# Where the transposed keys of one batch are copied, and in which order the first half of the work is issued

## The chip, the cores and the metric

The kernel runs on one core of a Trainium2 chip. The metric is the device time of one execution in microseconds. Before the change four runs gave a median of 235.56 us (234.56 to 236.28).

## The reference

Two stages are joined. The first is attention with 4 batches, 8 heads, 768 tokens and 64 numbers per head. Three heads ("retrieval") see all earlier tokens; the other five ("streaming") see the first 4 tokens and a window of 64. The second is a dense layer pair with a learned slope for negative values.

```python
stream_keep = causal & (is_sink | in_win)
mask = np.where(retr[0, :, 0, 0, None, None], full_mask, stream_mask)
scores = np.where(mask[None, :, :, :], scores, -1000000000.0)
a = np.exp(scores)
a = a / (np.sum(a, axis=-1, keepdims=True) + 1e-09)
...
x = np.ascontiguousarray(attn_out.transpose(0, 2, 1, 3)).reshape(B * S, H * D)
h = x @ w_in
g = np.maximum(h, 0.0) + alpha * np.minimum(h, 0.0)
return (g @ w_out).astype(np.float32)
```

`w_in` is 512 x 2048, `w_out` 2048 x 512, and `x` has 3072 rows.

## The kernel before

The attention is cut into 16 **segments** of two heads each: segment n belongs to batch n // 4 and holds the pair PAIRS[n % 4] (line 99). The four batches follow each other, and the dense layers of a batch run beside the attention of the next. The work is written as named items, and one long list, ORDER (lines 14 to 71), says in which order they are issued. Each engine runs its own instructions in the order of this list and waits at each for what it needs; so an item that is late holds up all that is behind it on its engine. The names are:

- `Lq5`, `Lk5`, `Lv5`: loads of a segment's queries, keys and values, from SyncE's (SP's) DMA queue. `Cq`, `Ck`, `Cv`: their casts to bf16. Lines 300 to 302 give the engine of each by a letter: P is GpSimd (POOL), A ScalarE (ACT), V VectorE (DVE). For segments 0 to 5 most are on GpSimd.
- `Tq5`, `Tk5`: transposes on TensorE (PE) into a PSUM bank, for segments 0 to 7 (`to_array`, line 354). `tq5`, `tk5.0`, `tk5.1`: copies of these to SBUF, for each head of the keys (`put_q`, line 364, `put_k`, line 372). Segments 8 to 15 are transposed by DMA.
- `S5.0.1`: a part of the scores on PE (lines 410 to 427 and 498), `s5.0.1` its exp on ScalarE (lines 466, 514, 520), `m5.0.1` the mask after it on VectorE. `A5.0`: the product with the values on PE (line 553), `a5.0` its division (lines 563 and 564). `X5`, `x5`: transpose of the result and copy to xT.
- `P0.4`: columns of the first dense layer, x @ w_in (`P1`, line 589). t = 0, 2, ... are the 512 tokens at the head of a batch, t = 1, 3, ... the other 256. P0.0 to P0.5 are cut in three, so that they can start before all heads are ready. `p0.4` is the negative part (relu with a factor of -1 on ScalarE, line 603, written to neg), `g0.4` the rest on VectorE (line 610), which gives the bank back to PE.
- `O0.1.2`: a quarter of the second layer for 128 tokens (`P2`, line 614), `o0.1` its copy and store. `L` and `l` are the last ones.
- `wi0` to `wi7`: loads of w_in, `wo0` to `wo3`: loads of w_out, all issued by GpSimd (lines 704 to 711). wi0 and wi1 hold the first 512 columns (f = 0 to 3), wi2 and wi3 the next (f = 4 to 7), and so on, half of the rows in each.

PSUM has eight banks. An item that needs one takes the bank that has been free longest, by the order of the list (`take`, line 145), and waits for whoever read it last.

In `put_k` a retrieval head's keys are one copy of 64 x 768 (line 385). A streaming head's are three: a large one of 64 x 744 (line 389) and two small ones (64 x 20, line 390, and 64 x 28, line 391). For segments 1 to 3 all are on VectorE. For segments 4 to 7, batch 1, the large copy of head 0 is on ScalarE, all others are on VectorE.

Scores of segments 4 and later are collected and issued in a burst (`emit_burst`, line 414): the two heads of a pair lie in different halves of the array's rows, and when each half has 576 columns or more, their matmuls are mixed (line 427), so that they run at once; else each runs alone (line 420). What stands between two score items in the list decides which scores come into one burst (`beside_burst`, line 431).

Of the kernel before, what the change touches and what calls it, by code (L numbers as in the profile page):

```python
# [25 lines left out]
p0.10 s5.0.1 s4.0.0 S4.1.5 S4.0.5 g0.8 Lq6 g0.10 S4.1.0 S4.0.3 nz1 p1.12 g1.12 p0.13 s4.1.0 s4.0.3 P0.15 Ck6.0 Lv5
S4.0.4 kfz0 P1.6 g0.13 p0.7 g0.7 Ck7.0 S5.1.0 ms s4.0.4 O0.1.0 Ck6.1 mr Cv5 S5.1.1 s4.1.5 s5.1.0 S4.0.1 S5.0.2 s4.0.5
S4.1.1 m4.1.5 p0.15 s5.1.1 P0.14 P0.12 s5.0.2 s4.1.1 O0.1.1 p1.6 p0.14 g0.15 s4.0.1 kfz3 P1.14 S4.1.4 S4.1.2 g1.6
S4.0.2 g0.14 Lk8 S5.0.0 S4.1.3 p0.12 s4.0.2 m5.0.2 g0.12 s4.1.3 m4.1.0 m5.1.1 O0.1.2 s4.1.2 Lq8 Tk7 m4.0.0 P1.10 Tk6
s4.1.4 O0.0.0 Lv7 O0.1.3 Cq6 Tq6 m5.0.1 tk7.0 tk7.1 p1.14 m4.0.1 O0.3.0 p1.10 O0.0.1 tk6.1 g1.14 Lv4 g1.10 Cv4 Ck8  # L30
s5.0.0 Lv6 m5.1.0 Lk9 O0.3.1 m4.1.3 tq6 m4.0.4 tk6.0 S6.1.2 S6.0.5 o0.1 m5.0.0 S7.0.1 m4.1.4 S6.1.0 S5.1.2 S7.0.2
O0.0.2 m6.0.2 Cq8 s6.1.0 O0.3.2 A5.0 s6.1.2 m4.0.3 Dk8.0 s5.1.2 Cv7 O0.3.3 m14.0.2 ns O0.0.3 m5.1.2 A5.1 s7.0.1 a5.0
m4.0.5 a5.1 o0.3 s7.0.2 A4.0 O0.2.0 s6.0.5 o0.0 X5 S6.0.0 S7.1.2 S6.0.3 a4.0 S7.1.0 S6.0.4 S6.1.1 O0.2.1 x5 s6.1.1 Ck9
S6.0.1 S6.0.2 O0.2.2 s6.0.4 m6.1.0 m4.1.1 s6.0.3 S7.1.1 Lq9 S7.0.0 s6.0.1 s7.1.0 m4.0.2 Dq8 A4.1 O0.2.3 O1.1.0 Cv6
s7.1.1 Dk8.1 m7.0.2 s6.0.0 nr o0.2 Cq9 S8.0.2 S8.0.0 O1.1.1 m6.1.1 s7.1.2 m7.1.0 s6.0.2 m6.0.1 s8.0.2 s8.0.0 a4.1
s7.0.0 S8.1.5 m7.0.1 S8.0.4 S8.0.3 m6.0.5 S8.1.3 m6.0.4 m6.0.0 m7.1.2 m6.1.2 S8.1.4 S8.0.1 s8.0.3 O1.1.2 m6.0.3 s8.0.4
m8.0.0 S8.1.0 m7.0.0 A6.1 A6.0 O1.1.3 a6.1 s8.0.1 m7.1.1 s8.1.3 Dk9.0 a6.0 Dk9.1 A7.1 a7.1 s8.1.4 A7.0 a7.0 Dq9 O1.0.0
Lq11 s8.1.5 X6 X4 Lq10 x4 x6 m8.1.3 S9.1.0 S9.0.0 kfz2 X7 s8.1.0 O1.0.1 x7 near0 m8.0.1 s9.0.0 Cq10 o1.1 s9.1.0 S8.0.5
S8.1.1 S9.0.1 m9.0.0 S9.0.2 S8.1.2 S9.1.2 s9.0.2 P2.13 s9.0.1 Lk10 P3.4 s8.1.2 s8.0.5 Cq11 m8.0.5 m9.0.1 Lv8 p2.13
P2.7 near2 p2.7 P2.3 P2.1 g2.13 p2.3 m8.0.3 s9.1.2 Ck10 O1.0.2 s8.1.1 Lv9 Lk12 m8.1.4 g2.3 g2.7 p3.4 Dq10 Cv8 Dk10.1  # L40
P2.4 P2.0 g3.4 p2.4 m8.1.5 m8.0.4 p2.1 P2.5 p2.0 m8.1.0 g2.4 S9.1.1 P2.8 P2.9 p2.5 P2.2 Dk10.0 Lk11 g2.1 p2.9 g2.5
g2.0 Dq11 A8.0 g2.9 P2.6 Lv11 O1.0.3 near1 m8.1.1 p2.2 p2.8 a8.0 g2.8 P2.14 Lv10 P2.11 s9.1.1 p2.6 g2.2 p2.14 m9.1.1
o1.0 S10.1.2 S10.1.0 S10.0.1 g2.6 S10.0.5 S10.1.1 g2.14 S10.0.2 s10.0.5 m9.1.2 s10.1.1 p2.11 P2.15 Cv9 m9.0.2 s10.1.2
P3.14 s10.0.2 s10.1.0 P3.2 Lq12 Lk13 O2.2.0 A8.1 Ck12 Ck11 m9.1.0 Dk11.1 g2.11 S10.0.3 S10.0.4 p2.15 s10.0.1 p3.2
s10.0.4 g3.2 P2.10 A9.1 s10.0.3 g2.15 p2.10 P3.8 A9.0 m10.1.2 a8.1 g2.10 m10.1.1 m10.0.5 m10.0.3 p3.8 P2.12 Lq14
Dk11.0 P3.6 m10.0.1 P3.10 Dk12.1 a9.1 Cq12 p3.6 p3.10 m10.1.0 O2.2.1 P3.12 O2.2.2 g3.8 p3.14 a9.0 O2.1.0 O2.1.1 g3.6
g3.10 p2.12 p3.12 S10.0.0 O2.1.2 S11.1.1 S11.1.0 g3.14 S11.0.1 g2.12 S11.0.0 m10.0.4 s10.0.0 P3.0 Cv10 X8 Lq13 s11.0.0
m10.0.0 s11.1.0 m11.1.0 p3.0 s11.0.1 s11.1.1 O2.1.3 A10.0 Ck13 Dq12 S11.0.2 O2.3.0 s11.0.2 S11.1.2 o2.1 O2.0.0 Cv11
g3.0 s11.1.2 m11.0.1 Dk12.0 Cq13 Dk13.0 m11.1.1 g3.12 O2.2.3 O2.0.1 a10.0 m11.1.2 A10.1 A11.1 a10.1 m11.0.0 O2.0.2
O2.0.3 Dk13.1 a11.1 m11.0.2 S12.0.1 S12.1.4 o2.2 S12.1.0 S12.0.0 o2.0 A11.0 O2.3.1 s12.0.1 Dq13 S13.1.1 S13.1.0 a11.0  # L50
S12.0.4 s12.1.0 S12.1.2 S13.0.1 s12.1.4 m12.1.4 s12.0.0 S13.0.2 X9 X10 s13.1.1 X11 s12.0.4 s12.1.2 s13.1.0 x11 O3.1.0
Lk15 O2.3.2 m13.1.1 S12.0.3 S12.0.5 S12.0.2 s13.0.2 S12.1.1 m13.1.0 m12.0.4 s13.0.1 S12.1.5 S13.1.2 O3.1.1 s13.1.2
P4.0 s12.1.5 s12.0.2 Cq14 P4.11 P4.1 Lq15 m12.1.5 p4.11 Lk14 O2.3.3 p4.0 s12.0.5 m12.0.1 p4.1 s12.1.1 O3.1.2 s12.0.3
Ck15 m12.0.2 g4.11 P4.13 O3.0.0 g4.0 P4.12 P5.6 m13.1.2 p4.13 Ck14 Lv13 Lv15 g4.1 g4.13 p4.12 m12.0.3 P4.4 P5.2 g4.12
# [20 lines left out]
def kernel(  # L75
# [296 lines left out]
    def put_k(key, n, hh, both=False):  # L372
        h = heads(n)[hh]
        T = row_tokens(n, h)
        rows = slice(64 * hh, 64 * hh + 64)
# [4 lines left out]
        if put[key] == 1 + both:  # L380
            give(held.pop(key))
        if RETR[h]:
            cuts = [0, -(-256 // T), S // T] if n == 0 else [0, S // T]
            for lo, hi in zip(cuts, cuts[1:]):
                copy(kt[:, 0:S].rearrange("d (p t) -> d p t", t=T)[:, lo:hi, :], src[:, lo:hi, :])
# [3 lines left out]
        copy(slots[:, 0:6, a:last, :], src[:, first:z, :].rearrange("d (j m) t -> d j m t", j=6))  # L389
        nc.vector.tensor_copy(slots[:, 6, a:a + S // T - z, :], src[:, z:S // T, :])  # L390
# [466 lines left out]
```

## Time and profile before

| what | value |
|---|---|
| median of four runs | 235.56 us |
| the profiled execution | 235.06 us |
| its span, first to last instruction | 233.3 us |
| TensorE clock granted | 1.00 |
| ScalarE neg, 128x512 (line 603) | 96 times, 611 ns |
| VectorE g, 128x512 and 128x256 (line 610) | 742 and 474 ns, 64 each |
| VectorE kT, 64x768, 64x744, 64x20, 64x28 | 956, 924, 170, 179 ns |
| ScalarE kT, 64x768, 64x744 | 804, 778 ns |
| ScalarE, smallest activation (128x96, line 516) | 269 ns |

The profile is of one execution. Busy time is a share of an engine's span; an instruction's duration overlaps a little with the next one's, so the step from one start to the next is shorter where an engine has work waiting. "A <- B" in a list of waits means that A's engine stood idle until B had ended. The chain of waits goes back from the last instruction: at each step to what released it. A line of it has the start, the length and what it was.

### The profile page before, as it was taken

To read this page: it belongs to the slowest core of one execution; us is meant where nothing else is said; L and a number is where in the kernel's file an instruction comes from. 1 tells how busy PE (TensorE), PEld (TensorE's weight loads), DVE (VectorE), ACT (ScalarE), POOL (GpSimd) and SP (SyncE) were. 2 spreads that over 40 slices of the span, in tenths; PEclk is the share of its full clock that TensorE was granted. 3 is DMA by queue.
4 is the path that set the end of the run, shared out by engine and by line. 5 is a ranking of instruction groups with operands and counts; after the bars stand their busy time and mean duration, and the time that the engine had idled before them with its cause. 6 is when DMAs were issued, how large, how long until landed. Compare 5 with 4: busy or idle time off the path is not lost.

```text
span 233.3 us, 5251 instructions
## 1 busy us (share of the span) xinstructions
PE 223.8 (96%) x2011; PEld 137.1 (59%) x2011; DVE 158.4 (68%) x409; ACT 136.0 (58%) x266; POOL 46.8 (20%) x95
## 2 busy tenths in 40 slices
PE   7798999989999999999999999999999999999994
PEld 6587757545656575556665546556764555554553
DVE  5776749698788797998977476978880245545110
ACT  6598419798856758677563864589422333623231
POOL 3679469002058110000001000010000020000000
PEclk9999999999999999999999999999999999999999
DMA  6999999999999999999959999680310130110033
GB/s 197 322 217 172 239 280 236 215 198 200 206 225 194 208 211 219 162 203 217 191 108 139 251 205 207 116 212 3 71 35 0 49 135 1 45 48 0 0 135 136
DMA packets 90833, 36.23 MB, mean 155 GB/s; under 512 B 77864, under 2 KB 89016, under 8 KB 90808
## 3 DMA queue, kind: packets, MB, share of 16 engines
q1 hardware_dynamic: 84616, 26.59, 58.9%
q0 software_dynamic: 5728, 8.91, 17.1%
q10 hardware_dynamic: 464, 0.40, 0.5%
q8 instruction: 15, 0.25, 0.5%
q14 instruction: 10, 0.08, 0.1%
HBM read 27.55 MB, written 6.29 MB: 145 GB/s over the span
## 4 chain that ended last, share of the span: by engine, by line
PE 77%; DMA 9%; DVE 6%; issue 2%; ACT 2%; POOL 1%; SPq 1%; DVEq 0%; POOLq 0%
PE P L618 33%; PE P L598 30%; PE P L553 5%; DMA w_in_b<-in_moe_w_in_dram 5%; DVE g L610 4%; PE P L427 3%; DMA qf<-in_q_dram 2%; DMA vf<-in_v_dram 2%; PE P L420 2%; PE P L637 2%; PE P L578 1%; DVE kT L389 1%; ACT neg L603 1%; PE P L362 1%; ACT qT L367 1%
## 5 line engine op out<-in xcount | busy, mean ns | idle before, releaser
L610 DVE SCALAR_TENSOR_TENSOR g<-neg,oma,P 128x512 bf16<-128x512 f32 (+1 forms) x128 | 72.1, 608 | 36.3 <-ACT neg L603 35.6
L598 PE MATMUL P<-xT,w_in_b 128*128 128x256 bf16 (+1 forms) x512 | 92.1, 326 | 1.0 <-DVE g L610 0.8
L603 ACT ACTIVATE neg<-P 128x512 f32<-128x512 f32 x96 | 55.8, 611 | 59.2 <-PE P L598 51.3
L618 PE MATMUL P<-w_out_b,g 128*128 128x512 bf16 x368 | 88.5, 379 | 0.0
L598 PEld LDWEIGHTS <-w_in_b 128*128 128x128 bf16 x512 | 48.5, 98 | 34.5 <-issue 2.2
L618 PEld LDWEIGHTS <-g 128*128 128x128 bf16 x368 | 34.5, 98 | 35.9 <-issue 0.8
L466 ACT ACTIVATE eR<-P 128x448 bf16<-128x448 f32 (+6 forms) x63 | 36.4, 630 | 7.7 <-PE P L459 3.1
L628 POOL DMA_DIRECT2D out_dram<-ot x18 | 10.4, 578 | 124.1 <-ACT ot L624 124.1
L624 ACT COPY ot<-P 128x512 f32<-128x512 f32 x23 | 13.2, 589 | 13.3 <-PE P L618 10.1
L564 DVE TENSOR_TENSOR xn<-P,rcp 128x448 bf16<-128x448 f32 (+1 forms) x32 | 19.4, 608 | 1.1
L520 ACT ACTIVATE eS<-P 128x384 bf16<-128x384 f32 (+1 forms) x25 | 13.6, 567 | 6.0 <-PE P L498 2.4
L514 ACT ACTIVATE eS<-P 128x352 bf16<-128x352 f32 x30 | 13.9, 488 | 4.2 <-PE P L420 2.3
L410 PE MATMUL P<-qT,kT 128*128 128x192 bf16 (+12 forms) x68 | 11.2, 251 | 1.3 <-ACT eR L466 0.8
L553 PEld LDWEIGHTS <-eS 128*128 128x128 bf16 x260 | 10.2, 97 | 3.4 <-issue 1.1
L553 PE MATMUL P<-vb,eS 128*128 128x65 bf16 x260 | 11.1, 193 | 0.9 <-POOL vb L310 0.9
L563 DVE RECIPROCAL rcp<-P 128x7 f32<-128x7 f32 (+1 forms) x32 | 6.3, 198 | 7.4 <-PE P L553 7.3
L529 DVE TENSOR_TENSOR eS<-eS,ms_near 128x352 bf16<-128x352 bf16 x30 | 9.8, 334 | 1.6 <-ACT eS L514 1.3
L347 POOL CAST vb<-vf 128x896 bf16<-128x896 f32 x6 | 5.6, 933 | 25.4 <-DMA vf<-in_v_dram 25.4
L553 PEld LDWEIGHTS <-eR 128*128 128x128 bf16 x276 | 9.7, 97 | 1.5 <-DVE xn L564 0.3
L553 PE MATMUL P<-vb,eR 128*128 128x65 bf16 x276 | 10.3, 193 | 0.1
L427 PE MATMUL P<-qT,kT 64*128 64x176 bf16 (+17 forms) x159 | 9.7, 247 | 0.4 <-DVE g L610 0.3
L427 PEld LDWEIGHTS <-kT 64*128 64x128 bf16 x159 | 6.3, 94 | 6.2 <-issue 5.4
(97 smaller groups left out, 189.4 us busy)
## 6 DMA issues: line engine op xcount, KB each, us to landing
out_dram<-ot POOLq DMA_DIRECT2D x18, 256.0 KB, 3.2
vf<-in_v_dram SPq DMA_DIRECT2D x22, 192.0 KB
kf<-in_k_dram SPq DMA_DIRECT2D x21, 192.0 KB
qf<-in_q_dram SPq DMA_DIRECT2D x18, 192.0 KB
qf<-in_q_dram SPq DMA_DIRECT2D x7, 384.0 KB
w_in_b<-in_moe_w_in_dram POOLq DMA_DIRECT2D x8, 256.0 KB, 9.5
w_out_b<-in_moe_w_out_dram POOLq DMA_DIRECT2D x4, 512.0 KB, 15.4
kf<-in_k_dram SPq DMA_DIRECT2D x9, 196.0 KB
```

The source lines that it names most:

```text
L410: nc.tensor.matmul(to, keys, queries, start=True, stop=stop)
L427: nc.tensor.matmul(to, keys[own], queries[own], start=True, stop=True)
L466: nc.scalar.activation(ebuf[n, hh][:, lo:hi].rearrange("p (x c) -> p x c", x=len(parts)), P[:, got[0]:got[0] + len(parts), 0:(hi - lo) // ...
L514: nc.scalar.activation(slots, sc[:, 0:352].rearrange("p (s c) -> p s c", c=176), AF.Exp, scale=scale)
L520: nc.scalar.activation(slots, sc.rearrange("p x (s c) -> p x s c", c=192), AF.Exp, scale=scale)
L553: nc.tensor.matmul(pav[:, i, :], e[:, o:o + 128], vv[:, j, hh, 0:D + 1], start=(m == 0), stop=(m == len(terms) - 1))
L564: nc.vector.tensor_tensor(xn[n][:, 0:nt, D * hh:D * hh + D], pav[:, :, 0:D], rcp.to_broadcast([128, nt, D]), op=ALU.mult)
L598: nc.tensor.matmul(psg[:, w * i:w * (i + 1)], w_in_b[:, c, 128 * fb:128 * (fb + 1)], xT[:, c, o:o + w], start=(x == 0), stop=(x == 3))
L603: nc.scalar.activation(neg[t, f], bank(held["P", t, f][0]), AF.Relu, scale=-1.0)
L610: nc.vector.scalar_tensor_tensor(g_buf[t % 2][:, fb, 0:w], neg[t, f][:, c], oma[:, fb:fb + 1], bank(got[0])[:, c], op0=ALU.mult, op1=ALU.add)
L618: nc.tensor.matmul(bank(held["O", t, s][0]), g_buf[t % 2][:, f, 128 * s:128 * (s + 1)], w_out_b[:, f, :], start=(f == 0), stop=(f == 15))
L624: nc.scalar.copy(ot, bank(got[0]))
```

## The change

In `put_k` all three copies of a key now use the engine of the segment: ScalarE for segments 4 to 7, both heads and small copies too, and VectorE for segments 0 to 3.

ORDER is another list up to the middle of batch 2 (lines 15 to 53); from the item P4.0 on it is as before. The same items are in it. The first lines of both, up to the first items of the second layer, and the code:

```diff
-kz0 id La zero Lq0.0 Lk1 kz1 vz0 Lk0 Lq1 Lq0.1 Lq3 vz1 sz0 Cq0.0 ro nmr qz0 kz2 kfz1 warm0 Ck1.0 Tq0.0 warm1 Ck1.1
-Ck0.0 Lq2 Tk0.0 warm2 tk0.0 tq0.0 Ck0.1 Tk0.1 S0.0.1 vz2 s0.0.1 idf Lk2 sz1 one Cq1 Cq0.1 Lv0 Tk1 S0.0.2 Lk3 Tq0.1
-s0.0.2 nms tk0.1 tk1.0 Lv1 Cq2 S0.0.0 s0.0.0 Tq1 tq0.1 tq1 S0.1.2 tk1.1 qz sz2 Ck2.0 S0.1.0 Ck2.1 Lv2 s0.1.2 wi0
-m10.0.2 Tq2 s0.1.0 Cv0 S1.0.1 s1.0.1 Tk2 S0.1.1 S1.1.0 vz3 vo Lv3 A0.0 s0.1.1 s1.1.0 S1.0.0 tk2.1 A0.1 tq2 Ck3.1 kz3
-tk2.0 Ck3.0 S2.0.0 a0.0 Tk3 a0.1 Cq3 s1.0.0 S2.1.0 wi1 s2.0.0 Cv1 s2.1.0 so X0 Lq4 wi3 wi2 S1.1.1 tk3.0 Tq3 x0 s1.1.1
-S2.0.1 tq3 A1.1 S2.0.2 tk3.1 s2.0.1 A1.0 a1.1 s2.0.2 Cv2 S3.1.0 s3.1.0 A2.0 S2.1.1 Cv3 a1.0 a2.0 Lk5 S3.1.1 X1 s2.1.1
-S3.0.0 Cq4 x1 A2.1 s3.1.1 S3.0.1 A3.1 a2.1 P0.1.0 wi5 s3.0.1 P0.0.0 a3.1 X2 s3.0.0 wi4 x2 P0.3.0 wi6 A3.0 a3.0 P0.0.1
-P0.3.1 wi7 P0.2.0 P0.1.1 Al Lk4 Ck5.1 P0.2.1 al X3 x3 Ck5.0 P0.4.0 P0.4.1 P0.5.0 P0.3.2 P0.2.2 p0.3 P0.5.1 P0.0.2
-P0.4.2 p0.2 Ck4.1 Lq5 Tk5 P0.5.2 Cq5 Lq7 g0.3 p0.4 g0.2 P1.0 P0.1.2 g0.4 tk5.0 tk5.1 Tq4 p0.1 g0.1 p0.5 wo0 wo1 P0.6
-tq4 Lk7 P1.4 P1.2 p0.6 g0.5 Tq5 p1.4 g0.6 p1.0 Ck4.0 g1.4 p0.0 Tk4 g1.0 Cq7 P0.9 p0.9 P1.8 g0.0 p1.2 Tq7 tq7 P0.11
-p1.8 tq5 P0.8 tk4.0 g0.9 p0.11 tk4.1 wo2 g1.2 p0.8 wo3 P0.10 g1.8 P1.12 nz0 S5.0.1 S4.0.0 P0.13 Ck7.1 g0.11 P0.7 Lk6
...
+Lq0.0 zero La id qz nmr Lk0 kz1 sz2 kz2 Ck0.1 vo Lk1 nms Ck0.0 qz0 Lq0.1 Lq1 kz0 Cq0.0 warm0 Tq0.0 warm1 sz1 tq0.0 Lq2
+vz0 Cq0.1 Tk0.0 warm2 tk0.0 Lk2 S0.0.0 sz0 s0.0.0 Tk0.1 S0.0.2 Lv0 vz1 Cq1 s0.0.2 Lk3 tk0.1 Tq0.1 S0.0.1 Ck1.0 s0.0.1
+Tq1 Ck1.1 vz2 Ck2.0 Tk1 ro Cq2 tq1 tq0.1 vz3 S0.1.1 S0.1.2 Ck2.1 s0.1.1 S0.1.0 Tk2 tk1.0 Cv0 tk1.1 s0.1.2 S1.1.1 Tq2
+s1.1.1 so Ck3.1 A0.0 Lv1 s0.1.0 S1.0.1 tk2.1 S1.1.0 tq2 idf tk2.0 kz3 Lv2 Ck3.0 Lq3 A0.1 Cv1 s1.0.1 wi0 m6.0.2 s1.1.0
+a0.0 S1.0.0 Tk3 S2.0.2 wi1 s1.0.0 Lv3 Cq3 a0.1 Lk4 X0 tk3.0 s2.0.2 wi2 Cv2 A1.0 S2.1.0 s2.1.0 x0 A1.1 a1.0 Cv3 S2.1.1
+a1.1 Tq3 s2.1.1 S2.0.1 Ck4.0 X1 tk3.1 Lq5 tq3 S2.0.0 Ck4.1 A2.1 Lk5 mr m4.0.2 s2.0.1 s2.0.0 S3.1.0 x1 A2.0 S3.1.1
+s3.1.0 a2.1 s3.1.1 S3.0.0 wi3 A3.1 wi4 s3.0.0 S3.0.1 s3.0.1 a2.0 Lk6 Tk4 Lq6 X2 a3.1 x2 A3.0 P0.3.0 tk4.0 P0.2.0 Al
+a3.0 X3 Ck5.0 Cq5 x3 P0.0.0 tk4.1 wi5 wi7 P0.0.1 P0.2.1 P0.3.1 P0.1.0 Tq5 al Lq4 wi6 P0.2.2 P0.1.1 Lq7 P0.3.2 P0.1.2
+P1.0 ms P0.0.2 p0.3 P0.5.0 P1.6 g0.3 tq5 Ck6.1 p0.1 P1.4 P0.5.1 Ck5.1 P0.5.2 p0.0 g0.0 Lk7 g0.1 p1.6 g1.6 p0.2 P0.6
+P0.4.0 Tk5 Lv5 p0.5 wo0 g0.2 one P0.4.1 g0.5 p1.0 p1.4 Cq4 g1.0 p0.6 P0.11 Ck6.0 Lq8 P0.4.2 P1.2 g0.6 wo2 tk5.0 nr
+tk5.1 nz0 g1.4 p1.2 Tq4 P1.8 m10.0.2 P0.10 S5.1.2 g1.2 wo1 p1.8 kfz0 p0.4 g1.8 Lk8 kfz1 wo3 p0.11 P0.14 g0.4 Cq6 P0.13
...
@@ put_k @@
-        copy = cast_of("A" if n >= 4 and hh == 0 else "V")
+        copy, small = (cast_of(x) for x in ("AA" if n >= 4 else "VV"))
...
         copy(slots[:, 0:6, a:last, :], src[:, first:z, :].rearrange("d (j m) t -> d j m t", j=6))
-        nc.vector.tensor_copy(slots[:, 6, a:a + S // T - z, :], src[:, z:S // T, :])
-        nc.vector.tensor_copy(slots[:, :, 0:a, :], src[:, 0:a, :].unsqueeze(1).to_broadcast([64, 7, a, T]))
+        small(slots[:, 6, a:a + S // T - z, :], src[:, z:S // T, :])
+        small(slots[:, :, 0:a, :], src[:, 0:a, :].unsqueeze(1).to_broadcast([64, 7, a, T]))
```

More of the change, by code (lines that the diff above doesn't have):

```diff
@@ L25 @@
-p1.8 tq5 P0.8 tk4.0 g0.9 p0.11 tk4.1 wo2 g1.2 p0.8 wo3 P0.10 g1.8 P1.12 nz0 S5.0.1 S4.0.0 P0.13 Ck7.1 g0.11 P0.7 Lk6
[L26 to L54, printed above, removed]
+Lq0.0 zero La id qz nmr Lk0 kz1 sz2 kz2 Ck0.1 vo Lk1 nms Ck0.0 qz0 Lq0.1 Lq1 kz0 Cq0.0 warm0 Tq0.0 warm1 sz1 tq0.0 Lq2
@@ new lines @@
+tq4 p0.14 kfz3 p0.10 P0.9 P0.8 g0.11 p0.13 g0.14 Tq6 p0.9 g0.10 g0.13 P1.10 g0.9 P0.12 tq6 p0.8 g0.8 Cq7 p0.12 P0.7
+p1.10 P1.14 S5.1.1 p0.7 s5.1.2 g0.12 O0.0.0 S4.1.1 S4.1.4 Lv4 p1.14 Lq9 S4.0.0 g1.10 s5.1.1 S5.0.0 g0.7 g1.14 S4.0.1
+kfz2 s4.0.0 s4.1.1 P0.15 s4.0.1 m4.0.0 Ck7.1 m5.1.1 P1.12 m4.1.1 s4.1.4 S4.0.4 S5.1.0 p0.15 g0.15 s5.0.0 S4.1.3 S4.0.2
+O0.0.1 s4.1.3 s4.0.2 S5.0.2 S4.1.2 Tk6 Cv5 m5.1.2 p1.12 O0.1.0 Cv4 s5.0.2 m4.1.3 Lk9 m5.0.0 Cq8 Ck7.0 O0.1.1 O0.1.2
+s4.0.4 s4.1.2 tk6.1 tk6.0 s5.1.0 Ck8 m4.0.4 O0.0.2 S4.1.5 S4.0.5 S4.0.3 S4.1.0 S6.1.2 m5.0.2 m4.1.4 s4.0.3 s4.1.0
@@ new lines @@
+s4.1.5 m5.1.0 O0.1.3 s6.1.2 g1.12 m4.0.1 Tq7 S5.0.1 O0.0.3 A5.1 s4.0.5 O0.3.0 O0.3.1 o0.0 Tk7 m4.0.3 m4.1.5 a5.1
+s5.0.1 m4.0.5 m4.1.0 tk7.0 O0.3.2 A4.0 m5.0.1 o0.1 A4.1 tk7.1 Lv6 a4.0 Dk8.1 Dq8 tq7 a4.1 O0.3.3 o0.3 A5.0 a5.0 Lv7
+S6.0.5 S6.1.1 S7.1.1 S6.0.4 S6.1.0 S7.0.0 s7.0.0 Cq9 Cv6 s6.1.0 O1.1.0 s6.0.4 s6.1.1 S7.0.1 S6.0.3 X5 nz1 O0.2.0
+m6.0.4 s6.0.5 s7.0.1 S7.1.2 S6.0.1 x5 O1.1.1 s6.0.1 Ck9 s7.1.1 O1.1.2 S6.0.2 S8.1.0 m6.0.1 s7.1.2 S7.1.0 m7.0.0 s6.0.3
+S7.0.2 S6.0.0 m6.1.2 S8.1.5 O0.2.1 O0.2.2 Dq9 m6.1.1 m6.0.3 Dk9.0 s6.0.2 m7.0.1 m7.1.1 s6.0.0 s7.1.0 Dk8.0 m6.1.0
@@ new lines @@
+m6.0.5 s7.0.2 m7.0.2 Cv7 m6.0.0 A6.1 O0.2.3 A6.0 O1.1.3 m7.1.2 Dk9.1 ns s8.1.0 m7.1.0 Lk10 o0.2 Lq13 o1.1 a6.0 A7.1
+A7.0 O1.0.0 Lv8 a6.1 S8.1.4 s8.1.4 O1.0.1 s8.1.5 S8.0.0 S8.0.3 S9.1.0 S8.1.1 a7.0 S8.1.3 a7.1 S9.0.1 Lk11 Lk12 S9.0.0
+O1.0.2 s8.0.0 Ck10 X6 s8.1.3 s8.0.3 s9.0.0 s8.1.1 Lv9 Lq10 s9.0.1 m8.0.0 X4 s9.1.0 O1.0.3 X7 S8.0.1 S8.0.4 x4 S9.0.2
+S9.1.2 x6 S8.1.2 o1.0 x7 m8.1.5 m9.0.0 m8.1.4 S9.1.1 S8.0.2 m9.1.0 s8.0.1 near2 s8.1.2 s9.1.1 s8.0.4 P2.5 s9.0.2 p2.5
+P2.14 P2.3 g2.5 S8.0.5 p2.3 Cv8 p2.14 P2.6 m8.1.0 P3.0 g2.3 P3.4 m8.1.1 P2.1 g2.14 p2.6 m9.1.1 s9.1.2 P2.0 p3.0 P2.13
@@ new lines @@
+g2.6 s8.0.5 m8.0.5 Lq11 m8.0.3 g3.0 p2.0 Ck11 P2.2 Dk10.0 m8.1.3 m8.0.1 m9.1.2 P2.11 p2.1 g2.1 g2.0 p2.13 p2.2 P2.8
+g2.13 Lq12 P3.10 p2.8 g2.2 p3.4 A8.1 P3.8 P2.15 near0 p3.10 g2.8 g3.4 p2.11 Cv9 Lk13 m8.0.4 A9.1 s8.0.2 a8.1 P2.7 Cq10
+P2.4 p2.7 g2.11 P3.6 g3.10 Cq11 A8.0 p2.15 g2.7 Dk10.1 P2.12 p3.6 Dk11.0 P3.14 p3.14 g3.6 O2.1.0 g2.15 a9.1 P2.10 p2.4
+Dq10 p2.10 Dk11.1 g3.14 Lv10 p2.12 Dq11 P2.9 g2.4 a8.0 g2.10 p3.8 O2.0.0 O2.0.1 p2.9 Lv11 X8 g2.12 S10.1.1 S10.0.0
+S10.0.5 S10.0.4 g2.9 s10.1.1 O2.1.1 m10.1.1 s10.0.5 s10.0.0 Cq12 near1 S10.0.2 S10.1.2 S10.1.0 S10.0.1 O2.0.2 s10.0.4
@@ new lines @@
+O2.0.3 m10.0.0 Ck13 s10.1.0 g3.8 S10.0.3 s10.1.2 s10.0.1 S11.0.1 S11.1.2 S11.1.1 S11.1.0 s10.0.2 m10.0.5 m9.0.1
+S11.0.2 s11.1.2 m10.0.4 Cv10 m10.0.1 Ck12 s10.0.3 m9.0.2 Dk13.1 m10.0.3 Cq13 O2.1.2 P3.2 O2.1.3 s11.1.0 m11.1.2 A9.0
+p3.2 Dq12 Cv11 s11.1.1 O2.2.0 g3.2 A10.0 Dk12.0 m10.1.2 m10.1.0 Dk12.1 S11.0.0 O2.2.1 a9.0 O2.2.2 s11.0.0 a10.0 Dk13.0
+m11.1.0 S12.0.4 Dq13 s11.0.1 A10.1 P3.12 m11.1.1 A11.1 s11.0.2 p3.12 Lq14 m11.0.2 a10.1 O2.3.0 m11.0.1 S12.0.2 m11.0.0
+O2.2.3 s12.0.4 o2.1 s12.0.2 o2.0 S13.1.1 S13.1.0 A11.0 g3.12 O2.3.1 S12.1.5 a11.1 S13.0.1 s13.1.0 S12.0.1 o2.2 a11.0
@@ L55 @@
+S12.0.0 s13.1.1 S12.1.0 S13.0.2 S12.1.4 s12.0.1 X9 O2.3.2 X11 s12.0.0 s12.1.0 s12.1.4 X10 m14.0.2 O3.1.0 s13.0.2
+s13.0.1 x11 m12.0.4 Cq14 S12.0.5 S12.1.2 s12.1.5 m13.1.1 m12.1.4 S13.1.2 m13.1.0 S12.1.1 S12.0.3 s13.1.2 O3.1.1
+s12.1.2 P4.0 Lk15 P4.11 P4.1 Lq15 m12.1.5 p4.11 Lk14 O2.3.3 p4.0 s12.0.5 m12.0.1 p4.1 s12.1.1 O3.1.2 s12.0.3 Ck15
+m12.0.2 g4.11 P4.13 O3.0.0 g4.0 P4.12 P5.6 m13.1.2 p4.13 Ck14 Lv13 Lv15 g4.1 g4.13 p4.12 m12.0.3 P4.4 P5.2 g4.12
 m12.0.0 p5.6 Cv13 o2.3 O3.0.1 Lv12 A13.1 O3.0.2 Dq14 P4.10 p4.4 p5.2 P4.7 Dk14.1 g4.4 a13.1 g5.6 m12.1.1 Cv12 p4.7
```

## The prediction

> **What bounds the kernel now.** I read the page first, then the table by stretches, then the chain of waits, then the timelines of single engines where the chain changes engine. The page says that TensorE is the bound:
>
> ```profile
> PE 223.8 (96%) x2011; PEld 137.1 (59%) x2011; DVE 158.4 (68%) x409; ACT 136.0 (58%) x266; POOL 46.8 (20%) x95
> ```
>
> The span is 233.3 us, so PE is idle for 9.5. The table by stretches (columns: PE, PEld, DVE, ACT, POOL busy, clock, DMA share, GB/s) shows where:
>
> ```profile
> 20.00:30.00 10.00, 8.60 (x152) 7.14 (x151) 7.79 (x20) 5.73 (x9) 6.76 (x13) 1.00 1.08 207
> 30.00:40.00 10.00, 9.85 (x92) 6.59 (x88) 7.06 (x17) 5.66 (x10) 8.16 (x14) 1.00 1.16 260
> 40.00:50.00 10.00, 8.78 (x60) 4.87 (x58) 7.94 (x17) 8.23 (x17) 0.65 (x2) 1.00 1.20 213
> 50.00:60.00 10.00, 10.00 (x80) 6.06 (x80) 8.72 (x26) 9.39 (x22) 1.72 (x4) 1.00 1.09 204
> 60.00:70.00 10.00, 9.72 (x87) 5.21 (x85) 8.65 (x27) 6.76 (x13) 3.31 (x9) 1.00 1.01 213
> ```
>
> From 70 us to the tail PE is busy all the time, the clock is full, and the DMA share is 1 or more in every row: only the first 66 us hold time to gain.
>
> Busy shares hide waits, because ends of matmuls are modelled. So I measure PE's **lag**: the start of an item, less the sum of the work ahead of it. A matmul counts (columns + 5.5)/2400 us; that is 0.216 for 512 columns (the chain has 0.86 for four), 0.109 for 256 (0.87 for eight), 0.056 for 128 (0.33 to 0.35 for six), and the larger half alone where two heads' scores run side by side. The lag is 8.5 us when the first expert matmul starts (28.12, work 19.66), 9.05 at the first score of batch 1 (45.41, work 36.36), 11.1 at P1.6 (50.97, work 39.88), 11.3 at 56.0, 12.1 at 67.56 (work 55.49). Afterwards no wait adds to it. So two losses lie beside the changed copies: 2.05 us at 45 to 50, and 0.7 at 62 to 65. The chain of waits names them:
>
> ```profile
> 20.82 0.60 POOL w_in_b L706
> 21.41 10.91 DMA w_in_b<-in_moe_w_in_dram
> ...
> 43.45 0.84 ACT qT L367
> 44.28 0.67 ACT kT L385
> 45.02 0.95 issue
> 45.97 1.66 DVE g L610 x4
> ```
>
> and the waits of VectorE in 33 to 66 us say the same from the other side:
>
> ```profile
> DVE kT L385 <- ACT kT L385: 2.0, 1, 2.0
> DVE kT L390 <- ACT kT L389: 1.3, 1, 1.3
> ```
>
> VectorE stands at its half of a transposed key until ScalarE has done the other half, and the g (prelu) operations that give PE its banks back stand behind it.
>
> **The copies.** Batch 1 is segments 4 to 7. VectorE loses the copies of head 1 (one of 768, three of 744) and five pairs of small ones (64x20, 64x28). On VectorE the steps from start to start are 0.96, 0.86 and about 0.29 for a pair: 0.96 + 3 x 0.86 + 5 x 0.29 = 5.0 us fewer. ScalarE gets four large ones at the step of its own row (44.12 to 44.81: 0.69), 2.8 us, and ten small ones that it has never run. The nearest ScalarE row is 128x96: 0.27 busy, but the next instruction starts 0.13 after it. Bounds: 1.3 (step) to 2.7 (busy). [...] The step decides here, since ScalarE is in a queue of work: 1.3. [...] Total 4.1 us more on ScalarE. Both copies of segment 4 now stand ahead of the first relu (neg), where ScalarE is idle for 5.54 us (28.4 to 33.96): 0.7 of the 4.1 costs nothing, and the other half's copy, which was in 34 to 66, leaves that stretch. Net there: 4.1 - 0.7 - 0.7 = 2.7 us. ScalarE's busy time over 40 to 70 leaves 30 - 24.4 = 5.6 us, so it fits, but 50 to 60 has 0.6 free. What queues behind the copies on ScalarE is negs and exps, and PE's banks wait for those. Adding ScalarE's steps (neg 0.48, exps 0.38 and 0.42, qT 0.68) from the first neg on, the latest of its due points in the new order (the bank of a score of segment 4, freed by the exp of S5.1.1) is 0.2 us ahead of PE, the rest some 0.7 to 2 us ahead; in the old order all are about 1 us ahead.
>
> **The waits.** With both halves and the small pieces on one engine the two waits above can't occur. The 2.0 us wait cost PE 2.05; the 1.3 us one 0.7. Both go, 2.75 us at most. What is late next is ScalarE (0.2 us of cover). I give back 0.3.
>
> **The order: DMA.** SP now issues k0 before k1 and q3 behind v2. Batch 0's twelve loads are still all ahead of v3, so v3 lands as before or little earlier: 26.12 before, 25 to 26 now (q3 and w_in pieces only change place); I take 25.5. What moves is w_in. Before, GpSimd issued the second column block (f 4 to 7) at 20.81 and 21.41; its pieces landed at 30.2 and 32.3, just ahead of P0.4.0 at 32.46. Now its second piece, wi3, stands behind the cast of v3 (0.93), its sink copies (0.63) and both casts of k4 (0.95). k4 follows v3 on SP's queue; before, the load behind v3 landed 1.9 after it, so 27.0 to 27.4. wi3 is issued at about 28.2. The earlier pieces took 5.4, 6.8, 9.4 and 8.4 us to land when first of a group; only the 9.4 had an older one ahead in the queue. I take between 6.8 and 8.4, as those saw the same full queues: 7.6, so 35.8; bounds 33.6 and 39.2 (the slower ones of a group took 10.9 to 12.4). [...]
>
> PE needs it at P0.5.0, which stands at work 25.83. P0.3.0 comes behind Tk4 (k4's transposes) and A3.0: 28.0 + 0.33 + 0.35 + 0.4 = 29.0 (lag 8.2), P0.5.0 5.1 later at 34.1. So PE waits 1.7 us, and the lag there is 35.8 - 25.83 = 10.0, against 9.05 before. The next pieces follow in the queue at 1.9 each (before: 37.2, 39.0, 41.0, 43.0): block 2 at about 39.6, due at 30.28 + 10.0 = 40.3; block 3 at 43.5, due at 44.5. w_out follows at 3.3 each: about 47, 50, 54, 57 for dues of 52, 55, 59, 61. v5 lands at 57 as before, due at 63.5. All covered, by 0.7 to 6 us; the ones of 0.7 and 1 are what goes first.
>
> **The order: PE.** The same 2011 matmuls run, but other scores stand side by side: 8 fewer run as half-array pairs (151 instead of 159). Summed by the larger half, scores of batches 1 to 3 take 12.08 us instead of 11.65: 0.43 lost, on PE's path and with no cover. From P4.0 on, the order is the old one.
>
> **Sum.** Lag before the steady part: 12.1. After: 10.0 + 0.3 = 10.3. So -1.8, +0.4 for the pairs: -1.4 us. The profiled execution took 235.06 (span 233.3 and 1.8 around it), so 233.7; the median of the four runs is 0.5 higher, 235.56, so **234.2**.
>
> **Rivals.**
> - *w_in lands soon* (33.6): P0.5.0 does not wait, lag 8.2; ScalarE then has its tight 0.2 us with no pause to catch up in, so I give 1.5 of what was lost back: 9.7. -2.4 + 0.4 = -2.0, 233.6; up to 0.9 better if ScalarE keeps up, 232.7. For it: the first pieces took 5.4 and 6.8. Against: they met fewer loads. Chance 0.15.
> - *w_in lands late*, slower. One mechanism: wi3 at GpSimd behind v3 and k4, PE in order at P0.5.0. It decides from a landing at about 37.2 (25.83 + 12.1 - 0.4 - 0.3), 9.0 us after issue. At 11.0 us, 39.2, the lag is 13.4: +1.3 + 0.3 + 0.4 = +2.0, 237.6. For it: 9.4 to 12.4 in the same trace; against: those with more than 10 had pieces ahead. Chance 0.28.
> - *ScalarE takes the place of VectorE.* Small copies at 0.27 and 0.2 us of cover: its exps come 1.4 later, the saved wait is given back, 235.5 (235 to 237). For it: 9.39 of 10 busy at 50 to 60. Against: PE's wait at P0.5.0 lets it catch up. Chance 0.15.
> - That the copies do not move can be ruled out: in the new program's order all 18 copies of batch 1's keys stand on ScalarE, and none on VectorE.
>
> **Numbers.** Main case 0.42, own range 233 to 235.3. A measurement of this kernel tells about 0.5% (1.2 us) from no change: below 234.4 is faster. Main case 0.30 faster and 0.12 same; early w_in 0.15 faster; ScalarE 0.10 same, 0.05 slower; late w_in 0.28 slower. Faster 0.45, same 0.22, slower 0.33. The range takes in the early end and most of the late one: 232.6 to 238.0.
>
> **What would show it.** No wait of VectorE's kT copies for ScalarE's. PE waiting at the L598 matmul at some 34 to 36 us, with w_in in the chain; if there is none, w_in landed soon. ScalarE near 10 of 10 in 50 to 60, and g waiting for neg. Small copies with steps near 0.13. PE without gaps from 66 us on. I am wrong if q3, now behind v2, delays the exps of segment 2 and 3 beyond 29 us, or if the order after 66 us has gaps of its own.

## The result, and the profile after

The changed kernel takes 233.31 us in the median of 43 runs (231.87 to 236.81), the kernel before 234.97 in 64 runs (233.93 to 240.03) of the same sessions. The ratio is 0.993 (95% interval 0.991 to 0.994): 1.7 us faster, where 1.4 was forecast. The profiled execution took 232.49 us, its span is 230.5 us, against 235.06 and 233.3 before. It is thus one of the quicker runs of the changed kernel, 0.8 under its median, while the profile of before lay at its own median. That difference returns below.

The page's first part, and the table by stretches (PE, PEld, DVE, ACT, POOL busy, clock, DMA share, GB/s), of the changed kernel:

```profile
PE 223.9 (97%) x2011; PEld 137.8 (60%) x2011; DVE 152.8 (66%) x395; ACT 139.9 (61%) x280; POOL 47.0 (20%) x95
```

```profile
20.00:30.00 10.00, 10.00 (x168) 8.24 (x166) 7.74 (x20) 7.60 (x11) 6.54 (x13) 1.00 1.11 238
30.00:40.00 10.00, 9.81 (x71) 6.14 (x70) 7.59 (x22) 6.78 (x14) 5.49 (x9) 1.00 1.17 255
40.00:50.00 10.00, 10.00 (x73) 6.29 (x72) 8.14 (x16) 9.66 (x20) 3.72 (x8) 1.00 1.21 200
50.00:60.00 10.00, 10.00 (x77) 5.16 (x76) 6.21 (x19) 9.15 (x22) 1.88 (x3) 1.00 1.11 213
60.00:70.00 10.00, 10.00 (x134) 6.64 (x133) 7.03 (x23) 7.86 (x20) 3.16 (x5) 1.00 1.23 237
```

PE's busy time is as before (223.9 against 223.8): the work is the same, and 2.8 us of waiting are gone. Three rows that had lost PE time (20 to 30, 40 to 50, 60 to 70) are full now; 30 to 40 still has 0.2 us missing. Fourteen instructions went from VectorE to ScalarE, whose row at 40 to 50 rose from 8.23 to 9.66.

The chain of waits of the changed kernel, where the GpSimd and DMA part of the start meets PE:

```profile
22.05 0.93 POOL vb L347
23.04 0.76 POOL vb L310 x2
23.80 0.86 POOL natm L332 x2
24.66 8.84 DMA w_in_b<-in_moe_w_in_dram
33.49 0.14 issue
33.63 4.07 PE P L598 x26
```

GpSimd casts v3, then k4, then issues wi3, and PE begins P0.5.0 as soon as it is there. The order of events is the forecast's, each some 2 to 3.5 us sooner. From 33.63 on the chain stays on PE. From 25 to 75 us PE has one wait:

```profile
PE P L598 <- DMA w_in_b<-in_moe_w_in_dram: 0.2, 1, 0.2
```

The waits of VectorE from 33 to 66 us in the changed kernel (what waited, for whom, us in total, times, longest) are these at the top:

```profile
DVE g L610 <- ACT neg L603: 4.3, 5, 1.6
DVE rcp L563 <- PE P L553: 2.3, 2, 2.0
```

No copy of a transposed key is in that list any more. VectorE waits for neg instead, but PE does not notice, as its lag shows. Measured by the same rule, in the profiles of the two kernels and of the experiments:

| kernel | lag at the start of expert work, us | lag at 42 to 45 | lag near 50 | lag near 67 to 75 | median, us |
|---|---|---|---|---|---|
| before | 8.5 | 9.0 | 11.1 | 12.1 | 234.97 |
| changed | 7.2 | 7.8 | 7.8 | 8.6 | 233.31 |
| copies only | 8.6 | 8.9 | 9.9 | 11.5 | 235.23 |
| order only | 7.4 | 7.6, then 9.3 | 10.5 | 11.5 | 235.48 |
| old order, all on VectorE | 9.0 | 10.4 | 11.6 | 15.1 | 236.87 |
| changed, small pieces on VectorE | 7.4 | 7.8, then 9.5 | 10.6 | 11.5 | 234.74 |
| changed, w_in late | 7.2 | 14.9 | 14.9 | 15.6 | 239.39 |
| new start, old rest | 6.9 | 15.2 | 15.4 | 17.2 | 241.46 |
| new to s8.0.4, old rest | 8.1 | 12.8 | 12.8 | 13.5 | 241.78 |

Each lag is of one execution. The medians of the experiments are to be read against the kernel before in their own sessions: 235.40 beside 1 to 4, 235.24 beside 5 to 8.

### The profile page after: what moved, and what is told of

It is laid out like the page before. It is cut to its first block, busy times and chain, and to the rows that moved or that the text cites. A ratio compares the mean times of both kernels' runs of the same rounds, so it can differ in the third digit from the quotient of the medians.

```text
span 230.5 us, 5254 instructions
## 1 busy us (share of the span) xinstructions
PE 223.9 (97%) x2011; PEld 137.8 (60%) x2011; DVE 152.8 (66%) x395; ACT 139.9 (61%) x280; POOL 47.0 (20%) x95
## 4 chain that ended last, share of the span: by engine, by line
PE 87%; DMA 6%; POOL 4%; DVE 1%; issue 1%; SPq 0%; ACT 0%; POOLq 0%
PE P L618 35%; PE P L598 34%; PE P L553 5%; DMA w_in_b<-in_moe_w_in_dram 4%; PE P L427 4%; PE P L420 2%; PE P L701 2%; DMA vf<-in_v_dram 2%; PE P L637 2%; POOL vb L347 1%; PE P L362 1%; PE P L578 1%; POOL w_in_b L706 1%; PE P L360 1%; POOL vb L310 1%
## 5 line engine op out<-in xcount | busy, mean ns | idle before, releaser
L598 PE MATMUL P<-xT,w_in_b 128*128 128x512 bf16 (+1 forms) x512 | 90.6, 326 | 0.2 <-DMA w_in_b<-in_moe_w_in_dram 0.2
L603 ACT ACTIVATE neg<-P 128x512 f32<-128x512 f32 x96 | 54.1, 605 | 59.3 <-PE P L598 51.5
L618 PEld LDWEIGHTS <-g 128*128 128x128 bf16 x368 | 34.0, 98 | 35.1 <-issue 1.1
L628 POOL DMA_DIRECT2D out_dram<-ot x18 | 10.1, 563 | 122.5 <-ACT ot L624 122.5
L410 PE MATMUL P<-qT,kT 128*128 128x192 bf16 (+14 forms) x68 | 11.3, 251 | 0.8 <-ACT eR L466 0.5
L553 PE MATMUL P<-vb,eR 128*128 128x65 bf16 x276 | 10.1, 193 | 0.0
L427 PE MATMUL P<-qT,kT 64*128 64x176 bf16 (+15 forms) x151 | 9.7, 251 | 0.0
## 6 DMA issues: line engine op xcount, KB each, us to landing
w_out_b<-in_moe_w_out_dram POOLq DMA_DIRECT2D x4, 512.0 KB, 11.6
```

Of the source, the lines that this page charges most:

```text
L410: nc.tensor.matmul(to, keys, queries, start=True, stop=stop)
L427: nc.tensor.matmul(to, keys[own], queries[own], start=True, stop=True)
L553: nc.tensor.matmul(pav[:, i, :], e[:, o:o + 128], vv[:, j, hh, 0:D + 1], start=(m == 0), stop=(m == len(terms) - 1))
L598: nc.tensor.matmul(psg[:, w * i:w * (i + 1)], w_in_b[:, c, 128 * fb:128 * (fb + 1)], xT[:, c, o:o + w], start=(x == 0), stop=(x == 3))
L603: nc.scalar.activation(neg[t, f], bank(held["P", t, f][0]), AF.Relu, scale=-1.0)
L618: nc.tensor.matmul(bank(held["O", t, s][0]), g_buf[t % 2][:, f, 128 * s:128 * (s + 1)], w_out_b[:, f, :], start=(f == 0), stop=(f == 15))
```

## The experiments

My theory after the result: the gain has two parts. The new start brings PE to the expert work with some 1.3 us less lag, and w_in comes just in time for it; and with all copies on ScalarE the two losses at 45 to 50 and 62 to 65 us do not occur. The rivals: that only the wait of VectorE for ScalarE mattered, not VectorE's load; that the order alone, or the copies alone, make the whole; that the start's gain came from GpSimd's and VectorE's fills of the v buffers, which stood ahead of loads; and that the landing of w_in is covered in any case.

**1. Copies alone.** The changed `put_k` with the ORDER of before.

```diff
-        copy = cast_of("A" if n >= 4 and hh == 0 else "V")
+        copy, small = (cast_of(x) for x in ("AA" if n >= 4 else "VV"))
...
```

> The old order with the new copies (all of batch 1's keys on ScalarE). Theory A, mine: what the change gains at 45 to 66 us comes from VectorE no longer standing at its half of a key until ScalarE has done the other half, so most of the 2.75 us of those two losses goes even in the old order; ScalarE has 3.4 us more work there, which takes back about 1: -1.0 to -2.0 us, ratio 0.991 to 0.996. Theory B: the copies by themselves bring nothing or cost, since ScalarE is the fuller engine there, and the new order makes the gain: 0 to +2 us, ratio 1.000 to 1.008.

Measured: 235.23 against 235.40 of the kernel before beside it, ratio 0.998 (0.995 to 1.0005): no difference that can be told. The loss at 45 to 50 us shrank from 2.05 to 1.05, but ScalarE now keeps PE waiting; PE's waits from 33 to 75 us in this kernel:

```profile
PE P L427 <- ACT kT L385: 0.8, 1, 0.8
PE P L420 <- ACT kT L385: 0.7, 1, 0.7
```

So in the old order the rival "ScalarE takes the place of VectorE" did happen: from the second to the last column of the table the lag still grows by 2.6 us (3.1 before), and 1.5 of that are these two waits. Alone, in the old order, the copies brought nothing that can be told.

**2. Order alone.** The new ORDER with the `put_k` of before.

```diff
-        copy, small = (cast_of(x) for x in ("AA" if n >= 4 else "VV"))
+        copy = cast_of("A" if n >= 4 and hh == 0 else "V")
...
```

> The new order with the old copies (head 1 and all small pieces on VectorE). Theory A: VectorE waits for ScalarE's half again at segments 5, 6 and 7, but segment 4's copies now stand ahead of the first relu, so only part comes back: 0.5 to 1.5 us of the gain of 1.7 is lost, ratio 0.995 to 1.000. Theory B: as fast as the changed kernel, ratio 0.992 to 0.994.

Measured: 235.48, ratio 0.997 (0.994 to 1.0005). Up to 40 us its lag is that of the changed kernel or less (7.4 to 7.6). Then it loses 2.9 us, and the timelines of VectorE and GpSimd in this kernel show at what:

```profile
38.69 2.90 DVE L332 CAST natm<-kf 128x384 bf16<-128x384 f32 x1
```

```profile
38.34 0.76 POOL L710 DMA_DIRECT2D w_out_b<-in_moe_w_out_dram  x1
39.10 1.28 POOL L673 TENSOR_SCALAR_AFFINE_SELECT mr_near<-one 128x1248 bf16<-128x1248 bf16 x1
40.30 0.91 POOL L292 MEMSET natk<- 128x960 f32 x1
```

The same in the changed kernel, VectorE first and then GpSimd:

```profile
38.76 0.35 DVE L332 CAST natm<-kf 128x384 bf16<-128x384 f32 x1
```

```profile
38.76 0.76 POOL L710 DMA_DIRECT2D w_out_b<-in_moe_w_out_dram  x1
39.52 1.28 POOL L673 TENSOR_SCALAR_AFFINE_SELECT mr_near<-one 128x1248 bf16<-128x1248 bf16 x1
```

One cast of 0.35 us took 2.90. It ends at 41.59, which is 0.38 after GpSimd's memset (41.21): as if it had run at its usual length once GpSimd had stopped. In the changed kernel it is over at 39.11, 0.4 us ahead of GpSimd's select. By the records the cast (38.69) started before the select (39.10), and it lasted through two instructions of GpSimd. The rows show the length and the overlap, not the reason; the cause stays open. Behind it stand g and, in turn, neg and PE (waits of PE for g: 2.0 us). The ratio lies in the range of my first theory, but no copy of a key waits for ScalarE in this trace: it got there by another way. So this run doesn't say what the new order is worth with the old copies: it lost to something that neither part of the change is about.

**3. The opposite of the copies.** Old ORDER, all keys of batch 1 copied by VectorE.

```diff
-        copy = cast_of("A" if n >= 4 and hh == 0 else "V")
+        copy = cast_of("V")
```

> The old order with all copies of batch 1's keys on VectorE, none on ScalarE. It takes the wait between the two engines away as the change does, but loads the other engine (3.4 us more on VectorE in 34 to 66). Theory A (the wait between the engines is the cost): faster than before by 0.5 to 1.5 us, ratio 0.994 to 0.998. Theory C (VectorE's load is the cost, the wait only its sign): slower by 1 to 2, ratio 1.004 to 1.009.

Measured: 236.87, ratio 1.006 (1.003 to 1.010). Here VectorE never waits for ScalarE's half of a key, and yet a loss of 1.2 us stays at 45 to 50 us, and a larger one comes at the scores of segment 6; PE's waits in this kernel, its longest line:

```profile
PE P L427 <- DVE kT L385: 2.8, 1, 2.8
```

That tells two ideas apart: if only the wait of one half for the other counted, this kernel would have gained. It is VectorE's whole queue, copies and g, that sets the time there. The profiled execution took 238.86 us, the longest of the nine, and already had 1.4 us more lag than that of before at 43 us, so only the growth after it, from 10.4 to 15.1, is read as the copies'; before, it grew by 3.0 in the same stretch.

**4. The fills.** In the old ORDER, `vz1 vz2 vz3` moved to stand behind `vz0`.

```diff
-zero ... vz0 Lk0 Lq1 ... vz1 ... vz2 ... vz3
+zero ... vz0 vz1 vz2 vz3 Lk0 Lq1 ...
```

> The old kernel with one edit of the order: the zero fills of the value buffers 1 to 3 (vz1, vz2, vz3 on VectorE) moved up behind vz0. In the old trace SP's next load of values went out at 13.63, just behind a fill at 13.08, and the values of segment 3 were there at 26.1; with the change at 22.0. Theory D (the fills hold the loads): v3 lands 1 us or more earlier and the lag at the first expert matmul falls by 0.5 to 1: -0.5 to -1.0 us, ratio 0.996 to 0.998. Theory E (the place of w_in's first piece and of q3 is what delayed v3): no change, 0.999 to 1.001.

Measured: 235.28, ratio 0.999 (0.996 to 1.002). The wait of the products of segment 3 for v3 (0.5 us before) is gone from its trace, but one of 0.9 us for v2 has come, and the time is the same. (Its profiled execution, 1.3 us over the median, began PE's work late; its lag is not used.) No gain of the fills alone can be told; the interval still allows one of 0.9 us.

**5. w_in late.** The changed kernel with `wi3` and `wi4` behind `Cq5`.

```diff
-... S3.0.0 wi3 A3.1 wi4 s3.0.0 ... Ck5.0 Cq5 x3 ...
+... S3.0.0 A3.1 s3.0.0 ... Ck5.0 Cq5 wi3 wi4 x3 ...
```

> The changed kernel with one edit: w_in's pieces wi3 and wi4 are issued behind the cast of segment 5's queries, some 6 us later on GpSimd (30.4 instead of 24.7). At the 7.5 to 9 us that pieces took to land, wi3 is there at 38 to 39.5. Theory A (the prediction's late rival: TensorE stands at P0.5.0, at work 25.83, until the piece has landed, and all of it stays): lag at P0.5.0 12.2 to 13.7 instead of 7.8; +4 to +5.5 us on the changed kernel, ratio to the kernel before 1.010 to 1.016. Theory H (later waits for other things would have come anyway, so a part is given back): lag the same at P0.5.0, but less than 4 us at the end, ratio 1.000 to 1.009.

Measured: 239.39, ratio 1.019 (1.014 to 1.024), more than either theory had. GpSimd waits for k5 first and issues wi3 behind it, at 30.7; PE gets it at 38.06. PE's waits in this kernel, and its table by stretches:

```profile
PE P L598 <- DMA w_in_b<-in_moe_w_in_dram: 4.6, 1, 4.6
```

```profile
34.00:36.00 2.00, 0.00 (x0) 0.00 (x0) 1.41 (x2) 0.44 (x1) 2.00 (x4) 1.00 1.35 228
36.00:37.00 1.00, 0.00 (x0) 0.00 (x0) 0.00 (x0) 0.00 (x0) 0.49 (x1) 0.81 1.29 192
...
42.00:43.00 1.00, 1.00 (x5) 0.45 (x4) 0.99 (x3) 0.00 (x0) 0.00 (x0) 0.50 1.22 195
43.00:44.00 1.00, 1.00 (x5) 0.40 (x4) 0.00 (x0) 0.63 (x2) 0.92 (x1) 0.77 1.21 196
```

Two things follow. The landing of w_in is PE's own path: nothing covers a later one. And it costs more than the wait. At P0.5.0 the lag is 38.06 - 25.83 = 12.2, so 4.8 us more than at P0.2.2; but at Tk5 it is 14.9. The other 2.7 us are the clock: in and after the idle stretch TensorE got half of it, 0.50 in the rows from 37 to 43, and the 5.4 us from 38.06 on at half the clock do 2.7 us less work. No later work gives any of it back (15.6 at 74 us against 8.9 in the changed kernel; the spans differ by 6.8).

**6. The small pieces.** The changed kernel with the copies of 64x20 and 64x28 on VectorE.

```diff
-        copy, small = (cast_of(x) for x in ("AA" if n >= 4 else "VV"))
+        copy, small = (cast_of(x) for x in ("AV" if n >= 4 else "VV"))
```

> The changed kernel with the ten small pieces of batch 1's keys on VectorE, the large copies on ScalarE. Theory A (VectorE's waits for ScalarE's copy are what costs, since relu's second halves queue behind them): of the 3 us of lag that the new order with the old copies lost at 40 to 48, half or more comes back: +0.7 to +1.8 us on the changed kernel, ratio 0.996 to 1.001. Theory C (VectorE's own 0.9 us copies are the cost): +0 to +0.4, ratio 0.992 to 0.995.

Measured: 234.74, ratio 0.996 (0.992 to 0.9995). The profiled execution has the lag of the changed kernel up to 43 us, and then the same long cast as order alone, 2.70 us from 38.96, beside GpSimd's select at 39.17. It says therefore nothing sure about the small pieces. It is inconclusive.

**7 and 8. Where the old list may take over.** The new start up to A3.0 (and both copies of segment 4) followed by the rest in the old order; and the new order as far as s8.0.4 followed by the rest of the old. Both with the changed `put_k`, and with the same items. The diffs show the seams.

```diff
-... a3.1 x2 A3.0 P0.3.0 tk4.0 P0.2.0 Al a3.0 X3 Ck5.0 Cq5 x3 P0.0.0 tk4.1 wi5 wi7 ...
+... a3.1 x2 A3.0 tk4.0 tk4.1 kfz1 one m10.0.2 Lq4 Cq4 P0.1.0 wi5 P0.0.0 P0.3.0 wi6 ...
```

```diff
-... m9.1.0 s8.0.1 near2 s8.1.2 s9.1.1 s8.0.4 P2.5 s9.0.2 p2.5 P2.14 ...
+... m9.1.0 s8.0.1 near2 s8.1.2 s9.1.1 s8.0.4 m14.0.2 s8.0.2 Lq11 m8.1.3 ...
```

> The new order up to the end of batch 0's attention (A3.0), then both copies of segment 4, then the old order of all that is left; the new copies. Theory A: the order of batch 0 (values earlier, queries of segment 3 later) is worth the 1.3 us of lag by which the changed kernel starts its first expert matmul sooner (7.2 against 8.5), and the rest of the gain is how the new order places the copies between relus: -1.0 to -1.8 us, ratio 0.992 to 0.996, lag about 7.3 at the first expert matmul, then losses of 1 us or more at 45 to 66. Theory F: only the part behind batch 0 counts, as the waits for w_in swallow an early start: 0 to -0.5 us, ratio 0.998 to 1.000.

Measured: 241.46, ratio 1.026 (1.021 to 1.031). The start's gain is there (lag 6.9 at the first expert matmul, less than in any other), and all is lost at once; PE's waits in this kernel:

```profile
PE P L362 <- POOL natm L332: 3.7, 1, 3.7
PE P L598 <- DMA w_in_b<-in_moe_w_in_dram: 2.4, 1, 2.4
```

and in GpSimd's timeline (in brackets the idle time ahead of an instruction, and what ended it):

```profile
35.97 0.82 POOL L319 CAST natq<-qf 128x768 bf16<-128x768 f32 x1 [9.98 <-DMA qf<-in_q_dram]
36.74 1.84 POOL L706 DMA_DIRECT2D w_in_b<-in_moe_w_in_dram  x3
38.55 0.99 POOL L332 CAST natm<-kf 128x384 bf16<-128x384 f32 x2
```

Two orders that don't fit at the seam: the old rest loads q4 late (`Lq4 Cq4` right behind it), GpSimd stands at that cast for 10 us, and the casts of k5, which PE needs next, stand behind. P0.4.0 also comes sooner in the old rest, and finds w_in not there, 2.4 us up to 33.55. After that wait the clock stayed at 1.00; behind the one of 3.7 us, at 39.65, it fell to half (0.50 at 40 to 42 us).

> The changed kernel with the new order kept up to the exps of segments 8 and 9 (s8.0.4), and the old order for what is left. By the sums of the larger halves this takes 0.44 us of TensorE's work away again, since scores of segments 10 to 13 stand in the old pairs. Theory A: that is on TensorE's path: 0.3 to 0.6 us faster than the changed kernel, ratio to the kernel before 0.989 to 0.992. Theory G: the pairs are hidden or the seam adds waits: 0.992 to 0.996.

Measured: 241.78, ratio 1.027 (1.022 to 1.033). Part of it lies at the seam: at 90 to 100 us PE is busy for 7.1 of 10 us, the chain there stands at a q load, and the clock is 0.70 in the next ten. So the later half of the new list is no free choice either. But the profiled execution, 244.04 us and the longest of the four, also shows something in the part that is the changed kernel's own order, in GpSimd's timeline:

```profile
25.46 0.50 POOL L332 CAST natm<-kf 128x384 bf16<-128x384 f32 x1 [1.26 <-DMA kf<-in_k_dram]
27.16 0.51 POOL L332 CAST natm<-kf 128x384 bf16<-128x384 f32 x1 [1.20 <-DMA kf<-in_k_dram]
27.61 1.22 POOL L706 DMA_DIRECT2D w_in_b<-in_moe_w_in_dram  x2
```

and in its table by stretches:

```profile
36.00:37.00 1.00, 0.09 (x1) 0.12 (x2) 1.00 (x2) 0.00 (x0) 0.00 (x0) 1.00 1.21 246
37.00:38.00 1.00, 1.00 (x8) 0.65 (x8) 0.06 (x1) 0.00 (x0) 0.00 (x0) 0.91 1.21 212
38.00:39.00 1.00, 1.00 (x6) 0.69 (x5) 0.00 (x0) 0.17 (x1) 0.68 (x1) 0.50 1.20 212
```

With the same list ahead of it, the last part of k4 landed at 27.16, where in the changed kernel's profile both casts were done by 24.7; wi3 was issued at 27.61 instead of 24.66, PE waited 2.3 us, and the half clock followed: lag 12.8 at Tk5 instead of 7.8. The mechanism of the slower rival is thus real, and an execution can fall into it without any change to this part of the list; why k4 was late is not shown. It seems to be one of the four: this one has a mean clock of 0.979, the others 0.985 or 0.986, which the stretch of 6.8 us at half clock behind the seam makes by itself (3.4 of 242 us). In the timed runs of the changed kernel a stretch at half clock is rare: the mean clock is 0.996 or more in all but one of them; that one had 0.991 and took 236.81 us, the longest.

## Why the prediction came out right, and what in it was wrong

The direction was right, and the gain of 1.7 us is near the 1.4 forecast, but the path of the main case was not: PE was to wait 1.7 us for w_in and waited 0.2, and the profile gained twice the forecast. That the medians lie so near it is in part luck. The time itself, 234.2, was 0.9 too high; 0.6 of this is that the kernel before takes 234.97 in 64 runs, and took 235.56 in the first four.

- **The waits that go: right.** The two waits of VectorE's copies are not in the list, and the rows of 40 to 50 and 60 to 70 us are full. From 45.4 to 67.6 us the lag grew by 3.0 before; from 42 to 67 it grows by 0.76 now. So 2.3 of the 2.75 us were kept. I had given 0.3 back to ScalarE; what came back is 0.5.
- **ScalarE: right in the changed order.** The full row came at 40 to 50 us (9.66 of 10) and not, as forecast, at 50 to 60 (9.15), and PE waits for no exp and no copy. The small copies last 0.17 to 0.19 us, less than the 0.27 of the nearest row of before; a pair with its gap costs 0.14 to 0.36, the five pairs 1.3 together, at the low end of the two bounds, as chosen. Copies alone showed that the rival is no idle one: in the old order ScalarE did hold PE up.
- **The DMA term: mis-sized.** I took v3 at 25.5, "as before or little earlier". GpSimd's cast of it begins at 22.05. SP issues v1 to v3 1.3 to 2.3 us earlier in the new list (10.48 to 16.86 us, before 11.81 to 19.15), which I had seen only as k0 and q3 changing place. Everything behind it moved: wi3 issued at 24.66 instead of 28.2. The landing took 8.8 us where I had 7.6 (all eight pieces 7.5 to 10.7), so it came at 33.5, not 35.8, and PE waited 0.2 us instead of 1.7. The lag at P0.5.0 is 7.8; I had 10.0, which is the step that failed. It is the case "w_in lands soon" that the profile shows, but not for its reason: the piece was slower than I took it to be, and was issued 3.5 us sooner.
- **The start of the expert work** was off with it: P0.3.0 at 27.96 instead of 29.0. The gain in lag of 1.1 to 1.6 us came in five kernels with the new start (6.9 to 7.4, against 8.5 before), so it isn't chance; only the one with the late k4 had 8.1.
- **The slower rival** had the right place and too low a price: I charged only the wait. For a landing at 39.2 I had given +2.0 us; at 38.06 the kernel was 4.2 us slower than that of before beside it (239.39 against 235.24), as half clock came with the wait.
- **The pairs.** 151 side-by-side matmuls, as counted; the 0.43 us of it can't be seen apart. The lags of the two profiles differ by 3.5 us at 67 and by 3.6 at 110, less 0.43 leaves 3.1, and the spans differ by 2.8; 0.3 is not placed.

So the profile gained 2.8 us in its span, twice the forecast, and the median only 1.7. The rest, about 0.8 us, is between this profile and its own kernel's other runs. Ten of the 43 took 234.4 to 235.5 us with a mean clock of 0.998 or more, which rules out a stretch of 3.4 us at half clock in them (it would take off 0.007), but not a wait for w_in: waits of PE of 2.4 and 2.8 us left the clock at 1.00 in two traces. So a landing some 2 us later would fit. A long cast near 38.7 us would fit too: the lag grew by 2.9 us with it in order alone and by 2.8 with the small pieces on VectorE, at mean clocks of 1.00 and 0.999, and it misses the changed kernel's profile by 0.4 us. It was seen in two other kernels with this order, not in this one. Which of the two it is stays open. Moving the select and the memset on GpSimd to a later place, with the copies as changed, as before, and with the small pieces on VectorE, would test the cast, and with it what the order and the small pieces are worth; it wasn't tried.

What each part is worth by itself stays open for the same reason. Copies alone and order alone gave -0.2% and -0.3%, each with an interval that reaches 0; together they gave -0.7%. That the copies need the order is supported by the two waits for ScalarE in the trace of copies alone, not by these ratios; whether the order needs the copies is not shown, since order alone lost to the long cast.

## What to carry to other kernels

When a step is moved, follow what it frees on each queue, down to when a load is issued, before any landing is taken "as before"; here loads that went out up to 2.3 us sooner on SP's queue let GpSimd issue the weights 3.5 us sooner than forecast, and the matmul that needed them waited 0.2 us instead of 1.7. Unloading one engine onto another brought nothing in the old order, where the second engine then kept PE waiting for 1.5 us; each half of such a change should be looked for in the other's queue. A wait of TensorE of over 2 us can cost more than its length (with w_in late, 4.6 us of wait and another 2.7 at half clock; waits of 2.4 and 2.8 us left the clock at 1.00), so the clock in the rows behind it belongs to its price.
